# Reordering w_out's pieces and moving the last small weights of a RetNet + ELU-MLP kernel

## The chip, the cores and the metric

One core of one Trainium2 chip. The metric is the device time of one execution in microseconds (us). The eleven executions of the kernel before in one batch took 650.78 to 654.57 us. All runs told of here were classed as fast, and kernels are compared within one batch of runs on one chip. A ratio is the mean time of one kernel's fast runs over that of the other kernel's fast runs of the same rounds, so it is not quite the ratio of the medians quoted beside it.

In the profile's lines PE is TensorE's matmuls, PEld its weight loads, DVE VectorE, ACT ScalarE, POOL GpSimd, and SPq the DMA queue, as its sequencer (SP) issues it. Two names in these lines need care: gT is the tile T3, and the sums ss of the last combine (explained below) lie in tiles called wi, as GpSimd's small weights do; VectorE's adds wi<-so are ss. gC is a tile of the hidden layer. A stretch is called throttled where the records show TensorE's clock at half.

## The reference, cut to what matters

```python
# B, H, S, D = 4, 8, 768, 64;  3072 tokens, d_model 512, d_ff 2048
for t in range(S):
    state = gamma * state + k[t] (x) v[t]
    y[t] = q[t] @ state / sqrt(D)
h = x @ w_in                                  # x: the y of all heads, 3072 x 512
g = np.where(h > 0, h, np.exp(np.minimum(h, 0)) - 1)
return g @ w_out
```

## The kernel before

The tokens go in six blocks of 512. Block 0 multiplies plainly (plain_first, plain_second) while the weights are decoded and sums of weights for Strassen products are formed. Block 1 uses one Strassen level in its first layer, in four "quadruples" n = 0 to 3 of seven products each (order 1, 2, 6, 7, 5, 3, 4), and two levels in its second. Blocks 2 to 5 use two levels more widely. The second layer's weights come back from DRAM through a ring of 11 tiles (wq).

Before, VectorE does the last combine's eight adds from 144.39 to 149.00 us and xt only from 150.12 on, behind two copies of outputs. The parts that matter (cuts are marked):

```python
def plain_second():                               # block 0, second layer: 8 pieces of w_out
    for f in range(NF):
        wo = decoded[2 * NQ + f]
        ...                                       # 8 matmuls into four banks "aabd"
        ...                                       # four adds: so;  DMA of so
        send_small()                              # DMAs of the small weights formed earlier
        sources = ...
        if f % 2:
            combine_w_out(f // 2, even, sources)  # second-level sums of an even and an odd piece
        even = sources
        yield
    for d in range(4):
        ot = hpool.tile([P, 2, TH], FP32, name="h", tag="h")
        eng(ot..., ops[d])                        # ScalarE for d = 0, 2, VectorE for d = 1, 3
        nc.sync.dma_start(out[0, ...], ot)

def combine_w_out(at, even, odd):                 # eight adds, eight DMAs of small weights
    if at < 3:
        ms = [mpool tiles];  ss = gq["T3"]...     # T3 is idle in block 0
    else:
        ms, ss = two tiles of the pool "stage"    # the raw pieces of w_in and w_out went through it
    ...                                           # ms from the decoded piece, ss from so

def second_twice(tb, behind_last):                # which tiles of the hidden layer a product reads
    quarter = lambda x, r, t: x.rearrange("p (f r) c -> p r f c", r=2)[:, r, :, P * t : P * t + P]

...
combine_x()                                       # xt: the inputs' sums, wanted by product 6
sides = itertools.chain(combine_w_in(1), combine_w_in(2)), combine_w_in(3), iter(()), iter(())
smalls = [], [], [3], [2]
for n in range(NQ):                               # block 1, first layer
    load(2 * CPB + n)
    ...                                           # products of quadruple n, with sides[n] between them
    for j in smalls[n]:
        combine_small(j)                          # GpSimd forms w_in's small weights (wi)
    send_small()
...
early.close()                                     # "stage" and its neighbour are given up
ring = ...;  for _ in range(RING): fetch_small()  # the ring lies where they lay
```

## Time and profile before

| | before |
|---|---|
| median of three runs | 654.61 us (653.89 to 654.94) |
| span of the profiled run | 653.4 us |
| TensorE busy, granted clock | 97%, 0.997 |
| VectorE, ScalarE, GpSimd busy | 76%, 37%, 6% |

TensorE is nearly always busy, so only its own waits and its throttled stretches can be won. The lines that carry this are in the prediction.

### The profile page before, as it was taken

How to read it: one execution, taken by the hardware profiler on the slowest of the kernel's cores; microseconds unless marked ns; L12 is line 12 of the kernel's file. 1: busy time of each engine (PE TensorE's matmuls, PEld its weight loads, DVE VectorE, ACT ScalarE, POOL GpSimd, SP SyncE). 2: the span in 40 equal slices, each digit the busy share in tenths (PEclk: the TensorE clock that was granted, in tenths of full speed). 3: DMA queues.
4: the chain of work that ended last, by engine and by line, in shares of the span. 5: the costliest groups of instructions: out<-in, count | busy, mean ns of one | idle time of the engine just before them, and what ended most of it. 6: DMA issues, size and time to landing. Idle time of an engine off the chain costs nothing.

```text
span 653.4 us, 15834 instructions
## 1 busy us (share of the span) xinstructions
PE 631.6 (97%) x6512; PEld 544.2 (83%) x6512; DVE 496.6 (76%) x887; ACT 240.8 (37%) x463; POOL 39.7 (6%) x38
## 2 busy tenths in 40 slices
PE   4999999998999999999999999999999899999998
PEld 3774445456889999988999989999988899988997
DVE  5789799998869776599767488867579958557976
ACT  6477541102643112556111465211454311356311
POOL 1001100000450000110000110000020000000000
PEclk9999999998999999999999999999999999999999
DMA  8648978979586789802789811698830688710694
GB/s 339 243 136 319 323 219 240 301 208 304 182 287 187 224 266 307 286 21 59 235 283 298 303 68 33 203 280 280 294 155 3 193 251 267 228 48 0 206 312 161
DMA packets 85208, 139.71 MB, mean 214 GB/s; under 512 B 6672, under 2 KB 38800, under 8 KB 82832
## 3 DMA queue, kind: packets, MB, share of 16 engines
q1 hardware_dynamic: 85136, 138.70, 65.6%
q8 instruction: 51, 0.84, 0.5%
q14 instruction: 21, 0.17, 0.1%
HBM read 114.56 MB, written 24.12 MB: 212 GB/s over the span
## 4 chain that ended last, share of the span: by engine, by line
PE 78%; DVE 11%; DMA 3%; SPq 3%; issue 2%; POOL 1%; ACT 1%; DVEq 0%; POOLq 0%
PE pa L797 18%; PE pa L758 10%; PE pd L797 9%; PE hp L451 6%; PE pb L797 5%; PE pa L712 4%; PE pb L758 4%; PE qa L758 3%; PE pd L712 2%; PE qd L758 2%; PE pd L758 2%; SPq L495 2%; PE y L338 2%; PE y L364 2%; PE kv L304 2%
## 5 line engine op out<-in xcount | busy, mean ns | idle before, releaser
L805 ACT COPY ms<-pa 128x128 f32<-128x128 f32 x104 | 27.7, 266 | 151.5 <-PE pa L797 149.8
L797 PE MATMUL pa<-ts,wq 128*128 128x128 f32 x560 | 74.1, 275 | 0.3 <-ACT ms L805 0.3
L797 PE MATMUL pd<-ts,wq 128*128 128x128 f32 x552 | 73.2, 276 | 0.0
L797 PEld LDWEIGHTS pa<-ts,wq 128*128 128x128 f32 x560 | 68.5, 192 | 0.8 <-ACT ms L805 0.5
L797 PE MATMUL pa<-gC,wq 128*128 128x128 f32 x480 | 65.9, 279 | 3.1 <-DVE gC L422 2.8
L797 PEld LDWEIGHTS pd<-ts,wq 128*128 128x128 f32 x552 | 67.2, 192 | 0.4 <-DVE res L809 0.2
L797 PEld LDWEIGHTS pa<-gC,wq 128*128 128x128 f32 x480 | 59.3, 192 | 4.9 <-DVE gC L422 3.5
L419 ACT ACTIVATE r<-r 128x512 f32<-128x512 f32 x96 | 60.5, 630 | 3.1
L418 ACT ACTIVATE r<-gC 128x512 f32<-128x512 f32 x64 | 39.9, 624 | 33.9 <-DVE gC L766 33.9
L809 DVE TENSOR_TENSOR res<-pd,ms 128x128 f32<-128x128 f32 x68 | 19.5, 287 | 38.3 <-PE pd L797 37.0
L247 POOL TENSOR_TENSOR kvn<-kvn,vf 128x512 f32<-128x512 f32 x22 | 25.6, 1170 | 357.4 <-DMA kvn<-in_qkv_dram 251.6
L422 DVE SCALAR_TENSOR_TENSOR gC<-r,gC 128x512 f32<-128x512 f32 x64 | 44.8, 732 | 0.7 <-ACT r L419 0.7
L674 DVE TENSOR_TENSOR ts<-gC,ts 128x512 f32<-128x512 f32 x60 | 41.3, 688 | 1.0
L674 DVE TENSOR_TENSOR ts<-gC 128x512 f32<-128x512 f32 x60 | 41.0, 683 | 0.2
L797 PE MATMUL pb<-gC,wq 128*128 128x128 f32 x240 | 31.7, 275 | 0.0
L465 PE MATMUL pa<-gC,w_s 128*128 128x512 f32 x64 | 30.6, 600 | 0.0
L830 ACT COPY res<-pa 128x128 f32<-128x128 f32 x34 | 9.1, 266 | 55.6 <-PE pa L797 54.1
L797 PEld LDWEIGHTS pb<-gC,wq 128*128 128x128 f32 x240 | 29.2, 192 | 0.4 <-DMA wq<-scratch_dram 0.4
L766 DVE TENSOR_TENSOR gC<-qa,gC 128x512 f32<-128x512 f32 x8 | 5.5, 692 | 25.4 <-PE qa L758 18.6
L538 ACT COPY m<-pa 128x512 f32<-128x512 f32 x24 | 13.9, 581 | 26.1 <-PE pa L758 12.6
L758 PE MATMUL pa<-xt,w_b 128*128 128x256 f32 x96 | 23.0, 382 | 0.0
L758 PE MATMUL pa<-xt,w_s 128*128 128x256 f32 x96 | 23.0, 382 | 0.0
(206 smaller groups left out, 1230.1 us busy)
## 6 DMA issues: line engine op xcount, KB each, us to landing
wq<-scratch_dram SPq DMA_DIRECT2D x277, 256.0 KB, 4.4
wraw<-in_w_dram SPq DMA_DIRECT2D x16, 1024.0 KB, 6.2
qk<-in_qkv_dram SPq DMA_DIRECT2D x24, 512.0 KB, 7.5
kvn<-in_qkv_dram SPq DMA_DIRECT2D x24, 512.0 KB, 8.1
scratch_dram<-w_s SPq DMA_DIRECT2D x8, 512.0 KB, 7.6
scratch_dram<-so SPq DMA_DIRECT2D x8, 512.0 KB, 6.0
out_dram<-res SPq DMA_DIRECT2D x14, 256.0 KB, 4.2
scratch_dram<-gT SPq DMA_DIRECT2D x12, 256.0 KB, 3.7
```

The source lines that it names most:

```text
L247: eng.tensor_tensor(out=kv[:, 1], in0=kv[:, 1], in1=vf[:, i].unsqueeze(2).to_broadcast([C, H, D]), op=ALU.mult)
L418: nc.scalar.activation(e, h, AF.Relu, scale=-1.0)
L419: nc.scalar.activation(e, e, AF.Exp, scale=-1.0)
L422: nc.vector.scalar_tensor_tensor(g, e, -1.0, h, ALU.add, ALU.max)
L451: nc.tensor.matmul(hp, lhsT=w[n][:, fi, j // 2, j % 2, :], rhs=xb[:, j, :], start=(j == 0), stop=(j == 3))
L465: nc.tensor.matmul(ops[d], lhsT=wo[:, row, (d if row else d ^ 2) * P :][:, 0:P], rhs=g_plain[row * NF + f], start=(f == 0 and row == 0), s ...
L674: sub = lambda o, x, y: nc.vector.tensor_tensor(out=o, in0=x, in1=y, op=ALU.subtract)
L712: nc.tensor.matmul(ps[:, f, :], lhsT=lhs[f], rhs=xs[j][k], start=(begin and f == 0), stop=True, skip_group_check=True,)
L758: nc.tensor.matmul(ps[:, fi, :], lhsT=w[:, fi, j2, :], rhs=x[:, j2, :], start=(j in (1, 7) and fi == 0 and j2 == 0), stop=(j2 == 1), skip_ ...
L797: nc.tensor.matmul(ps, lhsT=w[:, f, :], rhs=ts[j][k][:, f, :], start=(begin and f == 0), stop=(f == 3), skip_group_check=True,)
L805: nc.scalar.copy(m, ps)
L809: nc.vector.tensor_tensor(out=o, in0=x, in1=y, op=ALU.add)
```

## The change

The intent: in the second layer a product should read the low or the high tiles of the hidden layer rather than the even or odd ones, since the low ones are ready earlier. Then the second-level sums need piece f and piece f + 4 together, so the pieces are taken in the order 0, 4, 1, 5, 2, 6, 3, 7. Besides, the last combine's eight adds no longer stand in front of xt: ms is formed in block 1's first quadruple and ss in its fourth. combine_w_in(2) moves from the first quadruple to the second, so GpSimd, which needs its sums, starts later. Block 0's outputs leave through T3, so that the h tiles are free for block 1.

```diff
+    ORDER_F = [f for n in range(NF // 2) for f in (n, NF // 2 + n)]
-    quarters = lambda f: scratch.rearrange(...)[f % 2, f // 2]
+    quarters = lambda f: scratch.rearrange(...)[f // 4, f % 4]
...
-            if f % 2:
-                combine_w_out(f // 2, even, sources)
-            even = sources
+            if n == NF - 1:
+                held["last"] = combine_w_out(n // 2, low, sources)
+            elif n % 2:
+                for _ in combine_w_out(n // 2, low, sources):
+                    pass
+            low = sources
...
-            ot = hpool.tile([P, 2, TH], FP32, name="h", tag="h")
+            ot = gq["T3"][:, 2 * d : 2 * d + 2, :]
...
-        quarter = lambda x, r, t: x.rearrange("p (f r) c -> p r f c", r=2)[:, r, :, P * t : P * t + P]
+        quarter = lambda x, r, t: x[:, 4 * r : 4 * r + 4, P * t : P * t + P]
...
-    sides = itertools.chain(combine_w_in(1), combine_w_in(2)), combine_w_in(3), iter(()), iter(())
+    last = held["last"]
+    sides = [
+        itertools.chain(combine_w_in(1), itertools.islice(last, 4)),
+        itertools.chain(combine_w_in(2), combine_w_in(3)), iter(()), last,
+    ]
```

Cut: combine_w_out becomes a generator that yields after each add, and the host lays out w_out in the new order.

More of the change, by code (lines that the diff above doesn't have):

```diff
@@ L145, in prepare @@
         prepared.append((dst, todo))
-    quarters = lambda f: scratch.rearrange("(s k) p (f c) -> k f p s c", k=2, f=4)[f % 2, f // 2]
+    ORDER_F = [f for n in range(NF // 2) for f in (n, NF // 2 + n)]
+    quarters = lambda f: scratch.rearrange("(s k) p (f c) -> k f p s c", k=2, f=4)[f // 4, f % 4]
     def decode(fine=False):
@@ L174, in decode @@
         if n >= 2 * NQ:
-            nc.sync.dma_start(quarters(n - 2 * NQ)[:, 0:8], dst.rearrange("p (s c) -> p s c", c=P))
+            nc.sync.dma_start(quarters(ORDER_F[n - 2 * NQ])[:, 0:8], dst.rearrange("p (s c) -> p s c", c=P))
     def decode_all():
@@ L460, in plain_second @@
         ops = [bank(x).rearrange("p a b -> p (a b)") for x in "aabd"]
-        for f in range(NF):
-            wo = decoded[2 * NQ + f]
+        for n, f in enumerate(ORDER_F):
+            wo = decoded[2 * NQ + n]
             for row in range(2):
@@ L466, in plain_second @@
                         ops[d], lhsT=wo[:, row, (d if row else d ^ 2) * P :][:, 0:P], rhs=g_plain[row * NF + f],
-                        start=(f == 0 and row == 0), stop=(f == NF - 1 and row == 1),
+                        start=(n == 0 and row == 0), stop=(n == NF - 1 and row == 1),
                     )
@@ L495, in send_small, with combine_w_out @@
             nc.sync.dma_start(*to_send.pop(0))
-    def combine_w_out(at, even, odd):
+    def combine_w_out(at, low, high):
         tt = lambda o, x, y, op: nc.vector.tensor_tensor(out=o, in0=x, in1=y, op=op)
@@ L508, in combine_w_out @@
         ss = [ss[:, k] for k in range(4)]
-        for first, dst, e, o in ((0, ms, even[0], odd[0]), (3, ss, even[1], odd[1])):
-            a11, a21, a12, a22 = (x[:, :, P * d : P * d + P] for x in (e, o) for d in range(2))
+        for first, dst, k in ((0, ms, 0), (3, ss, 1)):
+            a11, a21, a12, a22 = (x[k][:, :, P * d : P * d + P] for x in (low, high) for d in range(2))
             s1, s2, s3, s4 = dst
             tt(s1, a21, a22, ALU.add)
+            yield
             tt(s2, s1, a11, ALU.subtract)
+            yield
             tt(s3, a11, a21, ALU.subtract)
+            yield
             tt(s4, a12, s2, ALU.subtract)
@@ L518, in combine_w_out @@
                 to_send.append((to[k, at], dst[k]))
+            yield
     def combine_w_in(n):
@@ L1203 @@
     w_out = _np.stack([w_out[0][:, :, ::-1], w_out[1]]).transpose(1, 2, 0, 3, 4).reshape(8, 128, 2 * DM)
+    w_out = w_out.reshape(2, 4, 128, 2 * DM).transpose(1, 0, 2, 3).reshape(8, 128, 2 * DM)
     w_bits = _np.concatenate([w_in, w_out], axis=0).view(_np.uint64)
```

## The prediction

> **What bounds the kernel now**
>
> I read the page first, then who waits for whom, then the timelines of TensorE, VectorE, ScalarE and the DMA queue around the three places that the change touches: the passage from the plain block 0 to block 1 (145 to 157 us), the passage from block 1's first layer to its second (183 to 205 us), and the same passage in one of the later blocks (302 to 316 us).
>
> The page: TensorE holds the end. It is busy in 97% of the span, and its row of slices has hardly a hole.
>
> ```profile
> PE 631.6 (97%) x6512; PEld 544.2 (83%) x6512; DVE 496.6 (76%) x887; ACT 240.8 (37%) x463; POOL 39.7 (6%) x38
> ...
> PE   4999999998999999999999999999999899999998
> ...
> PEclk9999999998999999999999999999999999999999
> ```
>
> 653.4 - 631.6 leaves 21.8 us in which TensorE is idle, so no reordering that only removes its waits can win more than that, plus what a throttled clock costs. In the list of waits (total, times, longest) only two of TensorE's entries can answer to this change; the larger DMA entry (7.5 us) is the start.
>
> ```profile
> PE pa L588 <- DVE xt L392: 2.9, 1, 2.9
> PE pa L797 <- DVE gC L422: 2.8, 4, 0.7
> ```
>
> The first is the passage into block 1. TensorE ends plain_second at about 145.2, does products 1 and 2 of the first quadruple, and then stands until VectorE has formed the input combinations xt. TensorE's timeline:
>
> ```profile
> 145.21 1.89 PE L588 MATMUL pa<-xb,w_a 128*128 128x256 f32 x8
> 146.93 1.89 PE L588 MATMUL pb<-xb,w_a 128*128 128x256 f32 x8
> 151.67 3.12 PE L588 MATMUL pa<-xt,w_s 128*128 128x256 f32 x8 [2.85 <-DVE xt L392]
> 154.59 2.47 PE L588 MATMUL pd<-xt,w_s 128*128 128x256 f32 x8
> 156.89 1.89 PE L588 MATMUL pa<-xt,w_b 128*128 128x256 f32 x8
> ```
>
> The reader is to see two costs: the gap of 2.85, and the two products after it, which start 2.92 and 2.30 apart where the next ones start 1.73 apart. In the table by stretches the one from 152.3 to 194.9 has a granted clock of 0.96: 0.04 x 42.6 = 1.7 us lost. So this place costs about 4.6 us.
>
> The second is the later blocks, four times 0.7 us: in block 2 the second outer product's first inner product stops three quarters through, until the activation of its last tile of C21:
>
> ```profile
> 308.88 0.83 PE L797 MATMUL pa<-gC,wq 128*128 128x128 f32 x6
> 310.40 0.49 PE L797 MATMUL pa<-gC,wq 128*128 128x128 f32 x2 [0.69 <-DVE gC L422]
> ```
>
> Third, a place that costs nothing now but is near an edge. At the end of block 1's first layer the DMA queue (SP, in order) sends one large tile of small weights (wi), waits until it has landed, and then starts filling the ring of second-layer weights:
>
> ```profile
> 177.69 0.38 SPq L102 DMA_DIRECT2D qk<-in_qkv_dram  x1
> 178.13 0.91 SPq L104 DMA_DIRECT2D kvn<-in_qkv_dram  x1
> 183.66 0.33 SPq L495 DMA_DIRECT2D scratch_dram<-wi  x1
> 187.54 0.80 SPq L652 DMA_DIRECT2D wq<-scratch_dram  x2
> ```
>
> The first wq is in at 190.1 (the trace's landing record, 2.6 us after its issue); TensorE needs it at 194.88, the first pa<-gC,wq. So there are 4.8 us of slack.
>
> [...]
>
> [...]
>
> [...] the ring's first fetch stands on SP from 183.99 to 187.54.
>
> [...] the T3 difference takes 0.69 us at 167.04 and 1.69 at 179.13, when GpSimd forms wi.
>
> **The change part by part**
>
> 1. Order of the pieces. The four input operands of a Strassen product are now halves of low and high tiles instead of even and odd ones. Counts and shapes of instructions, bytes and the strides' run length (128 elements) stay; so no busy time changes. What changes is readiness: low tiles come from quadruples 0 and 1, long done at the passage. In blocks 2 to 5 the stopped product reads C21 low and need not wait; the next product reads C21 high, its third tile is the late one, and by then it is nearly there (product 1 would end at 309.8, the third tile is used at about 310.2, the activation ends at 310.34). Gain about 0.6 of 0.69 each: 4 x 0.6 = -2.5 us.
>
> 2. The last combine (eight VectorE adds) leaves the passage into block 1. In VectorE's timeline they run from 144.39 to 149.00: 4 x 0.55 + 4 x 0.65 = about 4.6 us, all ahead of xt. Alone this would start xt at about 146 and close the gap of 2.85 and the throttle of 1.7.
>
> 3. But the block-0 outputs now go through T3 instead of free h tiles, and T3 still holds the third combine's small weights, which SP sends from 143.92 to 147.11. By the landing records its four parts are out at 147.2, 148.1, 149.0 and 150.0. Copy 0 (ScalarE, 0.59) can end at 147.8 rather than 143.4, and it frees the bank that product 1 wants: product 1 starts near 147.9 instead of 145.21. Copy 2 ends at 149.6; product 2 runs to 151.4. Copy 3 (VectorE, 0.68) can't start before 150.0, and ends near 150.6; two xt operations (0.72 and 0.68) end at 152.0. So product 6 starts at about 152.0, against 151.67. The wait moves from VectorE's adds to the landing. What may be saved is the throttle, as the idle time is split in two (2.6 and 0.6 us), or it may not. I put parts 2 and 3 together at -0.5 us (from -1.7 to +1.2).
>
> 4. The ss half of the last combine (4 x 128x512) is now in the fourth quadruple, n = 3, behind the previous quadruple's tail in VectorE's order. That tail ends at 192.6 in the present timeline (T1 difference 191.94 + 0.69), and VectorE then idles 3.06 us to 195.69:
>
> ```profile
> 191.94 0.69 DVE L600 TENSOR_TENSOR gC<-gC,gC 128x512 f32<-128x512 f32 x1
> 195.69 0.69 DVE L543 TENSOR_TENSOR h<-pd,m 128x512 f32<-128x512 f32 x1 [3.06 <-ACT m L538]
> ```
>
> VectorE has room for the four (2.6 us, 192.6 to 195.2). SP does not: the four sends of ss come ahead of wi and of the ring. Four sends, the last when the last add is done, 195.2 + 0.65 = 195.9; wi at 196.0 instead of 183.66; its landing 3.8 us later at 199.8 (183.66 to 187.49 now), rather later as 1 MB of ss goes ahead of it; ring fetch near 200.5; first weights near 203.2; half a us for VectorE's slower tail, since GpSimd's work is also pushed back by four adds. First product at 203.8 instead of 194.88: a wait of 8.9 us. Even with no wait for wi's landing it would be 196.4 + 2.6 = 199.0, thus 4.1 us. After it the clock is throttled: [...] 1.6 us, an estimate from the 1.7 above. Given back: the small waits that follow now (0.32 at 202.54 and the slow product before it), 0.7. Sum +9.8 us.
>
> 5. combine_w_in(2) moves from quadruple 0 to 1: four adds for four. Product 6 of quadruple 2 runs at 177.6, and its weights would be ready at about 171. Nothing on the path; GpSimd's wi starts about 4 us later than 171.38.
>
> Sum: -2.5 - 0.5 + 9.8 = +6.8; 654.6 + 6.8 = 661.4 us.
>
> **Rivals**
>
> A. The intended outcome: the passage's 4.6 us and the later blocks' 2.5 us are won and nothing new waits: 654.6 - 7.1 = 647.5. For it: VectorE has the idle time where the ops went, and the two waits are real. Against it: the DMA queue's in-order row at 183.66 to 187.54, with 4.8 us of slack against a push of at least 9 us.
>
> B. The stall at the ring is there but short, since the fetch needn't wait for wi's landing or since the tail of VectorE is earlier: +4.1 + 1.6 - 0.7 = +5.0, and if T3 costs nothing (its output copies find their parts landed) -4.6: with -2.5 the sum is -2.1, 652.5. Against it: the fetch does wait for wi now.
>
> C. All goes badly: T3 costs +1.2, the ring's wait is 11 us, [...] and nothing given back, block gains only 1.5: +13.3, 667.9. For it: ss moves 256 KB per send in pieces of 512 bytes, which lie ahead of wi and the wq in the same queue.
>
> **Range and chances**
>
> The middle is the sum, 661.4 us. The range of 8 in 10 spans half of B's and most of C's distance: 655 to 666.5. The line for faster by 2% is 641.5, below even A: 0.02. The line for slower by 2% is 667.7, about C: 0.07. Within 2%: 0.91.
>
> **What would show it right or wrong**
>
> Step 1: the four waits of pa on gC L422 fall from 2.8 us to under 0.8. Steps 2 and 3: xt no longer follows wi in VectorE's order; ScalarE's h copies are late and end on a landing from T3, and the first pa of block 1 waits for one of them. If product 1 still starts at 145.2 and product 6 within 149 to 150, step 3 is wrong and 4.6 us are won. Step 4: the first pa<-gC,wq of the second layer waits some 9 us for wq, the wi send on SP stands behind four small ones, and the granted clock drops a second time. If that product starts without a wait, step 4 is wrong and the result is near A.

## The result, and the profile after

| | before | after |
|---|---|---|
| median of four runs | 654.25 us | 662.62 us (660.26 to 664.06) |
| ratio | | 1.0132 (1.0091 to 1.0173) |
| span of the profiled run | 653.4 us | 658.5 us |
| granted clock | 0.997 | 0.989 |

The changed kernel is slower by 1.3%. The engines' busy time has not moved (TensorE 631.6 to 631.5 us); in TensorE's row of 40 slices the ninth has a small hole and the twelfth and thirteenth (181 to 214 us) a large one; in the thirteenth the clock dips too:

```profile
PE 631.5 (96%) x6512; PEld 544.5 (83%) x6512; DVE 497.0 (75%) x887; ACT 240.7 (37%) x463; POOL 40.8 (6%) x38
...
PE   4999999989966999999999999999999999999998
...
PEclk9999999999997999999999999999999999999999
```

TensorE's waits (total, times, longest). The two entries of before on xt and on gC are gone from this list, and two others stand in their place. Source lines have shifted: L599, L808 and L425 here are L588, L797 and L422 before.

```profile
PE pa L808 <- DMA wq<-scratch_dram: 9.8, 1, 9.8
...
PE pa L599 <- ACT gT L493: 2.5, 1, 2.5
```

**The passage into block 1.** TensorE's timeline of the changed kernel:

```profile
141.98 1.02 PE L468 MATMUL pd<-gC,w_s 128*128 128x512 f32 x2
145.49 3.62 PE L599 MATMUL pa<-xb,w_a 128*128 128x256 f32 x8 [2.49 <-ACT gT L493]
148.95 1.89 PE L599 MATMUL pb<-xb,w_a 128*128 128x256 f32 x8
150.68 1.89 PE L599 MATMUL pa<-xt,w_s 128*128 128x256 f32 x8
```

and the first copies into T3, ScalarE's and VectorE's:

```profile
144.85 0.58 ACT L493 COPY gT<-pa 128x512 f32<-128x512 f32 x1 [25.94 <-DMA scratch_dram<-gT]
145.74 0.69 DVE L493 COPY gT<-pa 128x512 f32<-128x512 f32 x1 [3.67 <-DMA scratch_dram<-gT]
```

Product 6 no longer waits for xt, but product 1 waits for a copy into T3, and that copy waits until the first small weights sent from T3 have landed (144.75 by the landing records). The first product after the gap takes 3.46 us to the next one's start, where 1.73 is usual: the throttle has moved with the gap (half clock from 145.41 to 148.83 in the records, from 152.33 to 155.74 before).

**The ring.** TensorE at the start of block 1's second layer:

```profile
190.61 1.89 PE L599 MATMUL pa<-xt,w_b 128*128 128x256 f32 x8
202.31 2.05 PE L808 MATMUL pa<-gC,wq 128*128 128x128 f32 x8 [9.80 <-DMA wq<-scratch_dram]
204.15 1.92 PE L808 MATMUL pb<-gC,wq 128*128 128x128 f32 x8
205.85 2.39 PE L599 MATMUL pa<-xb,w_s 128*128 128x256 f32 x8
```

The DMA queue in the same stretch:

```profile
178.36 0.33 SPq L502 DMA_DIRECT2D scratch_dram<-wi  x1
178.78 0.38 SPq L102 DMA_DIRECT2D qk<-in_qkv_dram  x1
179.22 0.91 SPq L104 DMA_DIRECT2D kvn<-in_qkv_dram  x1
191.41 3.21 SPq L502 DMA_DIRECT2D scratch_dram<-wi  x5
199.17 0.81 SPq L663 DMA_DIRECT2D wq<-scratch_dram  x2
```

Nothing is issued from 180.1 to 191.4 us: the queue stands at the first of the four ss sends. GpSimd's last wi, the fifth of the group, had been formed at 184.6 and waits behind them. The ring is fetched at 199.17 instead of 187.54; counted from the start of block 1 in each profile this is 14.0 us later, against a slack of 4.8.

**Where the time went.** The two kernels run the same 6512 matmuls in the same order, so the start of the same matmul can be subtracted between the two traces. The passage is counted from the end of plain_second to product 5 of the first quadruple (6.9 us of work), the quadruples from there to product 5 of the last one, the ring from there to the scores that follow the first five products of the second layer.

| stretch | before | after | difference |
|---|---|---|---|
| passage | 11.68 | 11.29 | -0.39 |
| quadruples | 36.26 | 36.49 | +0.23 |
| ring | 10.48 | 22.70 | +12.22 |
| waits on gC, blocks 2 to 5 | 2.8 | 0 | -2.8 |

These make +9.3 us. The two profiled spans differ by only 5.1, for two reasons outside the change: the profiled run of after reached block 1 2.4 us earlier, mostly since TensorE's slow start ended sooner (the first sixteen matmuls of plain_first start some 0.22 us apart there, and in the profile of before some 0.43 apart until 22.43 us; they take 3.72 us and 5.35), and the profile of before has some 2 us of TensorE waits in blocks 2 to 5 for which the profile shows no releaser; such waits of about a us also appear in profiles of other versions below. The medians differ by 8.4.

### The profile page after: what moved, and what is told of

Same layout as the page of the kernel before. It is cut to its first block, busy times and chain, and to the rows that moved or that the text cites.

```text
span 658.5 us, 15850 instructions
## 1 busy us (share of the span) xinstructions
PE 631.5 (96%) x6512; PEld 544.5 (83%) x6512; DVE 497.0 (75%) x887; ACT 240.7 (37%) x463; POOL 40.8 (6%) x38
## 4 chain that ended last, share of the span: by engine, by line
PE 83%; DVE 8%; DMA 3%; SPq 3%; issue 1%; ACT 1%; POOL 0%; DVEq 0%; POOLq 0%; ACTq 0%
PE pa L808 19%; PE pa L769 10%; PE pd L808 9%; PE hp L454 6%; PE pb L808 5%; PE pa L723 4%; PE pb L769 4%; PE pa L599 4%; PE qa L769 3%; SPq L502 3%; PE pd L723 2%; PE qd L769 2%; PE pd L769 2%; PE y L341 2%; PE kv L307 2%; DMA scratch_dram<-gT 2%
## 5 line engine op out<-in xcount | busy, mean ns | idle before, releaser
L808 PE MATMUL pa<-gC,wq 128*128 128x128 f32 x480 | 65.7, 281 | 9.8 <-DMA wq<-scratch_dram 9.8
L808 PE MATMUL pa<-ts,wq 128*128 128x128 f32 x560 | 74.1, 275 | 0.3 <-ACT ms L816 0.3
L808 PE MATMUL pd<-ts,wq 128*128 128x128 f32 x552 | 73.3, 276 | 0.1
L808 PEld LDWEIGHTS pa<-gC,wq 128*128 128x128 f32 x480 | 59.8, 194 | 11.5 <-issue 10.2
L808 PEld LDWEIGHTS pa<-ts,wq 128*128 128x128 f32 x560 | 68.5, 192 | 0.8 <-ACT ms L816 0.5
L808 PEld LDWEIGHTS pd<-ts,wq 128*128 128x128 f32 x552 | 67.1, 192 | 0.6 <-DVE res L820 0.5
L422 ACT ACTIVATE r<-r 128x512 f32<-128x512 f32 x96 | 60.5, 630 | 3.0
L425 DVE SCALAR_TENSOR_TENSOR gC<-r,gC 128x512 f32<-128x512 f32 x64 | 43.8, 716 | 0.7 <-ACT r L422 0.7
L808 PE MATMUL pb<-gC,wq 128*128 128x128 f32 x240 | 33.6, 282 | 0.1
L808 PEld LDWEIGHTS pb<-gC,wq 128*128 128x128 f32 x240 | 30.4, 197 | 0.8 <-DVE gC L425 0.8
L820 DVE TENSOR_TENSOR res<-pb,ms 128x128 f32<-128x128 f32 x36 | 10.3, 286 | 18.1 <-PE pb L808 18.1
```

The source lines that it names most:

```text
L422: nc.scalar.activation(e, e, AF.Exp, scale=-1.0)
L425: nc.vector.scalar_tensor_tensor(g, e, -1.0, h, ALU.add, ALU.max)
L808: nc.tensor.matmul(ps, lhsT=w[:, f, :], rhs=ts[j][k][:, f, :], start=(begin and f == 0), stop=(f == 3), skip_group_check=True,)
L820: nc.vector.tensor_tensor(out=o, in0=x, in1=y, op=ALU.add)
```

## The experiments

All ten kernels gave correct results. For each run the same three stretches, in us; "before" is the median of the runs of before in the same batch:

| run | us | before | ratio | passage | quadruples | ring |
|---|---|---|---|---|---|---|
| before (first profile) | | | | 11.68 | 36.26 | 10.48 |
| changed (first profile) | 662.62 | 654.25 | 1.0132 | 11.29 | 36.49 | 22.70 |
| e1_third | 661.79 | 652.45 | 1.0151 | 9.75 | 40.64 | 19.17 |
| e2_h_tiles | 661.96 | 652.45 | 1.0153 | 9.16 | 38.28 | 21.56 |
| e3_order | 649.55 | 652.45 | 0.9954 | 10.82 | 36.26 | 10.48 |
| e4_ss_late | 663.86 | 652.45 | 1.0179 | 9.56 | 36.36 | 22.39 |
| e5_t3 | 651.59 | 652.28 | 0.9989 | 9.60 | 36.35 | 10.48 |
| e6_ss_first | 650.79 | 652.28 | 0.9978 | 9.64 | 38.06 | 10.48 |
| e7_all_first_stage | 648.24 | 652.28 | 0.9933 | 6.91 | 37.98 | 10.48 |
| e8_gpsimd_late | 652.84 | 652.28 | 1.0006 | 9.81 | 36.60 | 10.48 |
| e9_ss_only_first | 646.73 | 653.48 | 0.9896 | 7.31 | 36.57 | 10.48 |
| e10_sends_late | 655.32 | 653.48 | 1.0039 | 9.61 | 38.06 | 13.79 |

A passage can include up to 1.7 us of throttle or none, in the same kernel: the executions of before list a granted clock of 1.0 in some runs and of 0.997 in others. Where it fell is said run by run. Source line numbers differ by a few from version to version.

### e3_order: the new order alone

The edit, on the kernel before: pieces in the new order, low and high tiles. The last combine stays in plain_second, the outputs in h tiles, the side work as before.

> Only the order of w_out's pieces and the split into low and high tiles, on the kernel before: the last combine stays in plain_second, the outputs in h tiles, the side work as before. Theory: the four waits of 0.7 us on the last activation of C21 go and nothing else changes: 2.7 us less, ratio 0.996. The gap of 2.85 us and the throttle at the passage into block 1 stay; the ring has no wait. Rival (the order of the pieces also changes when pieces of w_out are ready, and costs or wins some us in plain_second): the ratio differs from 0.996 by more than 0.004, and the stretch from 81 to 145 us has another length.

Measured: 649.55 against 652.45, ratio 0.9954 (0.9934 to 0.9974). The waits on gC are gone, the ring has none, plain_second takes 64.15 us as in the kernel before (so the rival fell), and the passage still has its wait on xt (1.99 us in this run, with a throttled stretch). The main part of the change is worth what it was meant to be worth, about 2.9 us.

### e4_ss_late: the four ss adds and sends alone

The edit, on the kernel before (cut: combine_w_out as a generator, whose first four adds, ms, still run in plain_second):

```diff
-    sides = chain(combine_w_in(1), combine_w_in(2)), combine_w_in(3), iter(()), iter(())
+    sides = chain(combine_w_in(1), combine_w_in(2)), combine_w_in(3), iter(()), held["last"]   # ss only
```

> The kernel before (even and odd tiles, h tiles for the outputs), with only the four ss adds of the last combine and their sends moved to the fourth quadruple. Theory: this alone makes the wait at the ring (9 to 10.5 us, with 2 us of throttle), about +12 us there; at the passage into block 1 four adds of 0.65 us less lie ahead of xt, so the gap of 2.85 us shrinks to some 0.3 us and the throttle goes, -4.2 us. Sum about +8 us, near 662 us. Rival (the wait at the ring needs the later wi of GpSimd as well, which this kernel does not have): the wait is below 5 us and the time below 656 us.

Measured: 663.86 against 652.45, ratio 1.0179 (1.0156 to 1.0202).

```profile
PE pa L810 <- DMA wq<-scratch_dram: 8.9, 1, 8.9
...
PE pa L601 <- ACT m L551: 2.4, 1, 2.4
```

The first line is the ring: 8.9 us without any of the rest of the change, and 11.9 us with throttle (22.39 against 10.48). So this move alone makes the loss. The second line is why the sum missed: I expected the passage to win 4.2 us, and it won 2.1. Four adds fewer let product 6 start on time, but then VectorE's next step waited 2.5 us for an h tile from which an output was still being sent, ScalarE's copy m came after that step, and TensorE's product 5 waited 2.4 us for the copy.

### e8_gpsimd_late: GpSimd's later start alone

The edit, on the kernel before, moves combine_w_in(2) into the second quadruple as the change does:

```diff
-    sides = chain(combine_w_in(1), combine_w_in(2)), combine_w_in(3), iter(()), iter(())
+    sides = combine_w_in(1), chain(combine_w_in(2), combine_w_in(3)), iter(()), iter(())
```

> The kernel before with one edit: combine_w_in(2) in the second quadruple, as in the changed kernel; nothing else. GpSimd's small weights then start and end 3 to 4 us later. Theory (the slack of 4.8 us at the ring takes this up): the ring is fetched 3 to 4 us later, no wait for wq above 1 us, time within 1 us of before. Rival (this delay is a cause of the wait at the ring): a wait for wq of 2 us or more with throttle, 655 us or more.

Measured: 652.84 against 652.28, ratio 1.0006 (0.9982 to 1.0030). Its DMA queue:

```profile
186.37 0.33 SPq L495 DMA_DIRECT2D scratch_dram<-wi  x1
190.41 0.80 SPq L652 DMA_DIRECT2D wq<-scratch_dram  x2
```

The ring is fetched 2.9 us later than before (2.1 counted from the start of block 1), and TensorE doesn't notice. GpSimd's delay alone is not the cause. It does take slack: the first weights are in at 192.93 and wanted at 194.08, 1.15 us where the kernel before had 4.8. Of the rest, 2.1 us are the later fetch; 1.5 us come from TensorE, which arrives earlier as this profile has no throttled passage.

### e6_ss_first: ss in the first quadruple

One edit, on the changed kernel:

```diff
-        chain(combine_w_in(1), islice(last, 4)),
-        chain(combine_w_in(2), combine_w_in(3)), iter(()), last,
+        chain(combine_w_in(1), last),
+        chain(combine_w_in(2), combine_w_in(3)), iter(()), iter(()),
```

> The changed kernel with one edit: the ss half of the last combine follows the ms half in the first quadruple; combine_w_in(2) stays in the second, so GpSimd's wi stays as late as in the changed kernel, and T3 stays. Theory (only the place of the ss sends in the DMA queue makes the wait at the ring; in the third quadruple they collided with GpSimd's work and the wi landed 9 us after its send): the sends are out by about 165 us, the ring is fetched some 4 us after GpSimd's last wi, TensorE's first product of the second layer waits under 1 us, the 10.2 us of throttle go: 12 us less than the changed kernel, 649 to 651 us here, ratio to before near 0.996. Rival (GpSimd's later wi is enough to make the wait): 3 us or more of wait for wq remain, 654 us or more.

Measured: 650.79 against 652.28, ratio 0.9978 (0.9949 to 1.0007). Its DMA queue:

```profile
184.86 0.33 SPq L502 DMA_DIRECT2D scratch_dram<-wi  x1
188.96 0.80 SPq L663 DMA_DIRECT2D wq<-scratch_dram  x2
```

The ring's stretch is back at 10.48 us with T3, the new order and GpSimd's delay all in place. With e4_ss_late this settles it from both sides: the place of ss makes the loss, alone and reversibly. The quadruples became 1.6 us longer, as VectorE now has twelve side adds in the first one.

### e1_third: ss in the third quadruple

One edit, on the changed kernel: `last` in the third place of sides instead of the fourth.

> The changed kernel with the last four adds (ss) and their sends in the third quadruple instead of the fourth; all else as changed. Theory (the DMA queue is in order, so the ring's first fetch stands behind sends that wait for VectorE): the fetch is issued near the place of the kernel before, some 5 us before TensorE needs it, the wait of 9.8 us for wq and the throttled stretch of 10.2 us both go, about 12 us less than the changed kernel, so near 651 us, ratio to before about 0.995. Rival 1 (the fetch is late because the four adds of combine_w_in pushed GpSimd's wi back): most of the wait stays, 658 us or more. Rival 2 (VectorE's slower adds beside GpSimd make the wait): about half of it stays.

Measured: 661.79 against 652.45, ratio 1.0151 (1.0123 to 1.0179). A miss: it is no faster than the changed kernel. The profile is of its slowest execution (664.78). VectorE, then the DMA queue:

```profile
182.54 1.75 DVE L506 TENSOR_TENSOR wi<-so 128x512 f32<-128x512 f32 x1
184.32 1.64 DVE L506 TENSOR_TENSOR wi<-wi,so 128x512 f32<-128x512 f32 x1
185.89 1.75 DVE L506 TENSOR_TENSOR wi<-so 128x512 f32<-128x512 f32 x1
187.56 1.52 DVE L506 TENSOR_TENSOR wi<-so,wi 128x512 f32<-128x512 f32 x1
```

```profile
184.32 5.71 SPq L502 DMA_DIRECT2D scratch_dram<-wi  x5
190.11 0.40 SPq L102 DMA_DIRECT2D qk<-in_qkv_dram  x1
190.56 1.22 SPq L104 DMA_DIRECT2D kvn<-in_qkv_dram  x1
191.87 1.05 SPq L502 DMA_DIRECT2D scratch_dram<-wi  x1
201.96 0.80 SPq L663 DMA_DIRECT2D wq<-scratch_dram  x2
```

An add that takes 0.69 us elsewhere takes 1.5 to 1.75 us here, while GpSimd is at work: on wi until 187.1, then on kvn. In the changed kernel, where GpSimd is done at 189.5, the same four adds take 0.68 to 0.69 us from 190.70 on. Here they end late; TensorE waits 3.5 us for VectorE's h (that is most of the longer stretch of the quadruples); and GpSimd's last wi, formed at 187.1, is sent at 191.87 behind four ss, another wi and two loads, and lands only at 201.8. The wait for wq is still 6.1 us of the 9.8, with 6.8 us of half clock in the records from 202.7 on. The time is rival 1's (658 or more), but its cause, GpSimd's delay, is ruled out by e6_ss_first; rival 2's slower adds are in the trace. This run doesn't speak against the cause, which e4_ss_late and e6_ss_first show, but my notion that any earlier place is free fell: here the adds ran beside GpSimd's work, at 1.5 to 1.75 us each, and the wi, behind the other transfers, landed 9.9 us after its send.

### e10_sends_late: adds early, sends late

The edit, on e6_ss_first: the four adds stay in the first quadruple, and their sends are held back to the end of the fourth.

```diff
+        if n == 0:
+            late = to_send[4:]
+            del to_send[4:]
+        if n == 3:
+            to_send.extend(late)
```

> The run with ss in the first quadruple, with one edit: VectorE's four ss adds stay in the first quadruple, but their four sends are held until the end of the fourth, in front of GpSimd's last wi, as in the changed kernel. It parts the two reasons that the sends have to delay the ring: the DMA queue waits for VectorE's adds, or the 1 MB of 512-byte pieces lies ahead of wi and the ring in the transfers. Theory (the wait for VectorE's adds): the four sends issue by about 182 us, wi as in the run it starts from, the ring is fetched at most 1.5 us later, the wait for wq stays under 1 us; within 1.5 us of that run, 651 us or so. Rival (the traffic): the wi lands 2.5 us or more later after its send, and 1 to 4 us of waiting for wq come back, with throttle, 653 us or more.

Measured: 655.32 against 653.48, ratio 1.0039 (1.0007 to 1.0070). Its DMA queue, then TensorE:

```profile
182.19 6.99 SPq L502 DMA_DIRECT2D scratch_dram<-wi  x5
194.77 0.81 SPq L663 DMA_DIRECT2D wq<-scratch_dram  x2
```

```profile
197.54 1.13 PE L808 MATMUL pa<-gC,wq 128*128 128x128 f32 x8 [3.07 <-DMA wq<-scratch_dram]
```

The rival was right here, but for the throttle, which did not come: 3.1 us of waiting are back though nothing waits for VectorE. By the trace's landing records the wi is issued at 186.6 and in at 194.6, 8.0 us, where it took 3.8 us in the kernel before and 4.05 us in e6_ss_first, whose queue holds the same loads there but no ss; a megabyte of loads and a megabyte of ss in 512-byte pieces (2048 of them in the changed kernel's trace) lie ahead of it. In the traces of before and of the changed kernel the transfers of this stretch land in the order in which they were sent (changed: ss from 193.75 to 196.53, wi at 199.03, the first wq at 202.07). So the 9.8 us of the changed kernel have two parts: some 3 us from the traffic, and the rest, some 6.7 us, from sends that wait for VectorE. This division is an estimate from this run, since the loads stand closer to the wi here than in the changed kernel; there the wi took 5.2 us, only 1.2 more than in e6_ss_first, so the traffic's part may be smaller. It also rests on GpSimd's delay: e6_ss_first fetches the ring 3.5 us later after the start of block 1 than the kernel before and has 0.9 us of slack left (first weights in at 191.66, wanted at 192.57), and 4.0 us more of landing make a wait of 3.1. With the 4.8 us of slack of the kernel before, the same traffic would by this sum not have been felt; no run tests that.

### e2_h_tiles: the outputs back in h tiles

One edit, on the changed kernel: `ot` is an h tile again.

> The changed kernel with block 0's outputs in h tiles again, as before, instead of T3. Theory (T3 is still being sent, and the copies out of PSUM wait for it): the first pa of block 1 starts right behind plain_second, the wait of 2.5 us goes and the throttle after it too, product 6 has its xt in time; 4.2 us less than the changed kernel, near 658.4 us. Rival (xt is held by something else, so that moving the outputs back wins nothing): within 1 us of the changed kernel, with another wait of 2 to 3 us in front of product 1, 2 or 6. The wait at the ring stays about 10 us in both.

Measured: 661.96 against 652.45, ratio 1.0153 (1.0129 to 1.0176): near the changed kernel, so the rival was nearer the truth. Product 1 starts on time as I expected, but VectorE then stops:

```profile
151.85 0.69 DVE L554 TENSOR_TENSOR h<-pb,m 128x512 f32<-128x512 f32 x1 [3.20 <-DMA out_dram<-h]
```

and TensorE waits 2.1 us in product 5, with a throttled stretch. The changed kernel's author had a reason to leave the h tiles: with them the wait is on their landing, with T3 on T3's.

### e5_t3: T3 alone

One edit, on the kernel before: `ot` in T3, as in the change.

> The kernel before with one edit: the outputs of block 0 go through T3. Theory (the copies wait for the landing of the sends from T3 at 147 to 150 us, and the xt operations follow them on VectorE anyway at about 149): product 1 of block 1 waits about 2.5 us with a throttle, xt is ready about 1 us later than now; the passage costs as much as before or up to 2 us more, 653 to 655 us. Rival (T3 is free in time): no wait in front of product 1, time as before.

Measured: 651.59 against 652.28, ratio 0.9989 (0.9960 to 1.0017), no difference. Product 1 waits 1.56 us for the copy and product 6 another 0.49 us for xt; no stretch is throttled in this profile. The waits are where the theory has them, but the first is shorter than the 2.5 us expected and brought no throttle.

### e7_all_first_stage: a third place for the outputs

The edit, on e6_ss_first: the outputs go into a tile of "stage" that nothing uses at that time.

```diff
+        ots = stage.tile([P, 4, 2, TH], FP32, name="ot", tag="stage")
-            ot = gq["T3"][:, 2 * d : 2 * d + 2, :]
+            ot = ots[:, d]
```

> As the run with ss in the first quadruple, and block 0's outputs in a stage tile that nothing is using, neither T3 (still being sent) nor h tiles (wanted by block 1 before the outputs have landed). Theory (both places of the outputs make a wait on a landing in the passage into block 1): no wait of TensorE between 140 and 160 us above 0.7 us and no throttle there; 4.0 to 4.6 us less than the run with ss in the first quadruple, near 645.5 us, ratio to before 0.989. Rival (a third wait appears in the passage, of VectorE or on the PSUM banks): within 2 us of that run.

Measured: 648.24 against 652.28, ratio 0.9933 (0.9909 to 0.9957). The passage is 6.91 us, its bare work, without a wait or throttle. By the medians of the same batch it is 2.5 us under e6_ss_first, not 4.0 to 4.6: I had counted on a throttle there, and e6_ss_first's profile had none. What is left is the longer quadruples:

```profile
PE pd L599 <- DVE h L554: 1.0, 2, 0.6
```

### e9_ss_only_first: only ss moves

The edit, on e7_all_first_stage: the ms half stays in plain_second, only the ss half goes to the first quadruple.

```diff
                 held["last"] = combine_w_out(n // 2, low, sources)
+                for _ in range(4):
+                    next(held["last"])
```

> The best run so far, with one edit: of the last combine the ms half (four adds of 0.5 us) stays in plain_second, and only ss moves, to the first quadruple. Theory: the first quadruple of that run holds four adds too many, which makes quadruples 1 to 3 1.7 us longer (36.25 against 34.53 us, two waits of TensorE on h of 0.5 us); this goes to under 0.4 us, and the passage still has no wait above 0.7 us, since xt is ready at about the time when products 1 and 2 end; 1.0 to 1.7 us less, near 646.8 us, ratio to before about 0.991. Rival (the longer quadruples come from the GpSimd overlap, not from the count of adds): no change, or the passage gets longer by 1 us and more.

Measured: 646.73 against 653.48, ratio 0.9896 (0.9870 to 0.9923). This beats both kernels. The quadruples are at 36.57 us, and what the passage pays is one short wait on TensorE:

```profile
147.46 1.97 PE L601 MATMUL pa<-xt,w_s 128*128 128x256 f32 x8 [0.17 <-DVE xt L395]
```

## Why the prediction was right

It gave 661.4 us (655 to 666.5) and slower by about 1%; the median is 662.62. By its own steps:

**Step 1, the order of the pieces (-2.5).** Right: the waits on gC fell from 2.8 us to none, and e3_order alone brings 2.9 us.

**Steps 2 and 3, the passage (-0.5).** Right in mechanism; that the size, -0.39, came so near is partly luck, since the profiles of both kernels hold a throttled stretch of 3.4 us in the passage. Without one the waits on T3 gave 9.60 us in e5_t3. Product 1 waited 2.49 us where 2.6 was worked out, for the copy behind T3's landing. Whether the throttle follows was left open in the text; it came in this profile and not in e5_t3, e6_ss_first and e10_sends_late, whose passages have the same two waits but shorter ones in front of product 1 (1.6 us). The length alone does not decide it, as the list at the end shows.

**Step 4, the ring (+9.8).** The mechanism was right, and e4_ss_late, e6_ss_first and e8_gpsimd_late show it; the sum was too small: it came to +12.2. The wait was 9.8 us, not 8.9; the throttle cost 2.3 us (4.55 us of TensorE's work after 202.31 ran at half clock), not 1.6; and the 0.7 us "given back" did not come, since the wait of 0.32 us after the first products is still there. The wait grew at the landing: from wi's send to the ring's fetch 4.5 us were allowed (196.0 to 200.5) and 5.4 passed (193.81 to 199.17), as the wi took 5.2 us to land instead of 3.8. The half us for VectorE's slower tail was right (0.5, counted from the start of block 1); from the last add to wi's send 0.8 us were allowed and 0.5 passed.

**Step 5, combine_w_in(2).** Right: no cost on the path (e8_gpsimd_late), though the ring's fetch comes 2.1 us later there, and 3.5 us later in e6_ss_first, out of 4.8 us of slack.

So the total is off by 1.2 us at the median, and by about 2.5 us in the parts that the change explains (+9.3 against +6.8), nearly all of it in step 4. Rival A, the intended outcome at 647.5, fell at the ring. It was in reach, though: with ss moved to the first quadruple alone and the outputs in a free tile the kernel lands there (e9_ss_only_first, 646.73).

Two small things in the working don't hold. 655 us lies at some 70% of the distance to B, not at half, which would be 657. 4 x 0.55 + 4 x 0.65 is 4.8; the 4.6 us are the stretch in the timeline, where the adds overlap a little. Of the clock, the records of before show the length of the loss (3.41 us at half clock, from 152.33 to 155.74), not its cause. And rival C's +13.3 counts 2.6 us of throttle at the ring, an estimate of mine (one and a half times the 1.7 us of the passage); the changed kernel's profile gave 2.3.

## What to carry to other kernels

Idle time of the engine that does moved work is not enough: ask where the transfers that depend on it stand in the DMA queue, and what stands behind them (here nothing was issued from 180.1 to 191.4 us, with a finished wi and the ring behind). A tile that was just sent was not written before its landing here (VectorE waited 3.67 us for T3 in the changed kernel, 3.20 us for h in e2_h_tiles), so a "free" buffer for outputs should be one whose last reader is long gone. When side work is spread over stages, put it where GpSimd is quiet (beside it an add of 0.69 us took 1.5 to 1.75), and well before a point where a memory pool is given up.

## What else the profiles show of the clock and of landings

- Gaps of 2.85 us (before), 2.49 us (changed) and 1.99 us (e3_order) were followed by 3.4 us at half clock, while 2.43 us (e4_ss_late), 2.65 us (e8_gpsimd_late) and 3.07 us (e10_sends_late) were not. So in these profiles a longer gap did not always throttle and a shorter one could; what decides it was not shown.
- The loss after a gap was not always 3.4 us long: after the 9.8 us of the changed kernel the records show half clock from 196.6 to 206.9 us, 4.55 us of it in TensorE's work.
- The same 1 MB send landed after 3.8 us in the kernel before, 5.2 us behind four ss sends (changed), 8.0 us behind these and two loads (e10_sends_late) and 9.9 us behind four ss, another 1 MB send and two loads (e1_third).
- At the point where the memory pool is given up, the ring's first fetch waited for the landing of the last wi in every version (183.66 to 187.49 us before), and in the changed kernel VectorE's first second-layer operation waited 5.2 us for the same landing.
